# Sigmoid attention and a gated FFN in one kernel: other places for the attention visits, other sums per FFN unit, another order at the start

## The chip, the cores and the metric

One core of a Trainium2 chip. The metric is the device time of one execution in microseconds (us); the profile's span, from the first to the last instruction, is about 1.8 us shorter. A time more than 1.5% above the fastest of the same kernel counts as slow and is left out. In this document PE is the matrix engine, DVE VectorE, ACT ScalarE, POOL GpSimd and SP SyncE.

## The reference

```python
# q, k, v: (8, 12, 448, 64); w_gate, w_val: (768, 1536); w_out: (1536, 768)
scores = q @ k.T / sqrt(64) - log(448)
attn   = sigmoid(scores) @ v                    # per batch and head
x      = attn.transpose(0, 2, 1, 3).reshape(3584, 768)
g      = x @ w_gate
out    = ((g * sigmoid(g)) * (x @ w_val)) @ w_out
```

## The kernel before

Everything is scheduled by hand on one core. Heads are taken four at a time, so there are 24 tile sets n (three in each of eight batches), each with seven score tiles c. A *visit* puts up to four score tiles and the PV product of a finished tile set between FFN units. An FFN1 unit (b, f) is 12 matmuls of 448 columns into the two banks of one PSUM tile, then a gate: sigmoid on ACT, two products on DVE, the last of which writes hT. PSUM is a ring of four such tiles, and a score tile, a PV product or an FFN tile takes the next place in the ring when its last reader is done. FFN2 works on pairs of batches with sums of hT (tiles S) and sums of w_out (tiles wT), so that seven products replace eight; the sums of hT are made on DVE two at a time after each unit of the odd batch.

```python
def ffn1(b, f):
    D = Banked("f", made=(b // 2, f))
    for prs in (range(NP - 2), range(NP - 2, NP)) if f == 0 else (range(NP),):
        ffn1_mm(D, b, f, prs)
    ffn1_gate(D, b, f)               # ACT: s = sigmoid; DVE: t = g * s, hT = val * t
    if b % 2:
        h_sums(b // 2, f)            # puts 1 or 3 sums into a queue
        make_sums(2)                 # does up to two of them
# ... (cut)
visits = [tiles[:2], tiles[2:4]]     # then 3, and from set 4 on 4 + 3 tiles
# ... (cut)
    frac = (j * C + c) / (NJ * C)    # place of a visit within its batch, by tiles
# ... (cut)
def attn_step(group, pvs, how):
    for part in (group[:2], group[2:]):
        scs = [(n, c, qk_tile(n, c)) for n, c in part]               # scores, PE
        rest = [pv(pvs.pop(0), how) for _ in range(len(pvs))]        # PV of the set before
        for i, (n, c, sc) in enumerate(scs):
            sig_tile(n, c, sc, split=len(group) == 4 and part[0] == group[0] and i == 1)
        for f in rest:
            f()
```

Loads, casts to bf16 (POOL, names `c<-st`) and transposes by DMA (`T<-c`) of later tile sets hang on the visits through a table.

## Time and profile before

| | before |
|---|---|
| times at first | 417.18, 417.66, 424.82 us (the last 1.8% above the first: slow) |
| span of the profile | 414.7 us |
| PE / DVE / ACT / POOL busy | 97 / 62 / 51 / 23% |
| first FFN1 matmul, end of the last matmul | 22.33 us, 410.3 us |
| matmuls | 3194 |

The prediction below shows the lines of the page and of the chain. They are read like this: PE holds the chain nearly alone, so only what holds up PE counts; but its busy time also covers waits, so the distance between starts is what has to be compared.

### The profile page before, as it was taken

The page shows a single profiled execution, that of the slowest core. Times are in us where ns is not written, and L with a number is a line of the kernel's source. Part 1 is how long each engine was busy: PE and PEld are TensorE (multiplying, and loading weights), DVE is VectorE, ACT ScalarE, POOL GpSimd, SP SyncE. Part 2 cuts the span into 40 slices and gives each one's busy share as a digit, 9 for nine tenths or more (in the row PEclk, how much of TensorE's full clock was granted, in tenths as well). Part 3 has the DMA queues.
Part 4 walks back from the last instruction along what each step waited for, and adds up shares of the span by engine and source line. Part 5 has one row for each costly group of instructions (what it writes and reads, how often), then busy time and mean ns, then how long its engine had stood idle before and what let it go on. Part 6 is the DMA issues. An engine that isn't in the chain of part 4 may idle for free.

```text
span 414.7 us, 7943 instructions
## 1 busy us (share of the span) xinstructions
PE 403.1 (97%) x3194; PEld 209.9 (51%) x3194; DVE 256.7 (62%) x472; ACT 213.5 (51%) x294; POOL 94.5 (23%) x125
## 2 busy tenths in 40 slices
PE   6799999999999999999999999999999999999995
PEld 3444545545555445445565445445555545555563
DVE  3637557778855555678554555568745447578653
ACT  5966986745444745745704865665715472222000
POOL 5528162446030643200030346020000000000000
PEclk9999999999999999999999999999999999999999
DMA  8999999986779985331374999340025400000135
GB/s 281 238 259 238 220 199 230 216 182 150 192 139 238 197 197 155 67 95 24 62 195 130 200 186 213 86 69 0 2 63 136 114 2 0 2 0 2 38 81 149
DMA packets 59845, 54.39 MB, mean 131 GB/s; under 512 B 35744, under 2 KB 53280, under 8 KB 59808
## 3 DMA queue, kind: packets, MB, share of 16 engines
q0 software_dynamic: 18880, 30.94, 33.9%
q1 hardware_dynamic: 40496, 22.62, 25.5%
q8 instruction: 25, 0.41, 0.4%
q10 hardware_dynamic: 432, 0.33, 0.3%
q14 instruction: 12, 0.10, 0.1%
HBM read 47.19 MB, written 11.01 MB: 140 GB/s over the span
## 4 chain that ended last, share of the span: by engine, by line
PE 89%; ACT 4%; DVE 3%; issue 2%; DMA 1%; POOL 0%; SPq 0%; DVEq 0%; ACTq 0%
PE ps_D L294 51%; PE ps_D L418 18%; PE ps_D L228 8%; PE ps_D L260 6%; PE ps_D L476 5%; ACT pt L246 3%; DMA st<-in_q_dram 1%; PE ps_D L198 1%; DVE S L377 1%; DVE t L314 1%; ACT s L312 0%; DVE hT L318 0%; ACT pt L243 0%; DVE T L204 0%; DVE xT L269 0%
## 5 line engine op out<-in xcount | busy, mean ns | idle before, releaser
L246 ACT ACTIVATE pt<-ps_D,sb_t 128x896 f16<-128x896 f32 x148 | 140.3, 1016 | 84.0 <-PE ps_D L228 79.3
L294 PE MATMUL ps_D<-xT,wg 128*128 128x448 f16 x576 | 126.6, 353 | 0.1
L294 PE MATMUL ps_D<-xT,wv 128*128 128x448 f16 x576 | 126.3, 352 | 0.0
L314 DVE TENSOR_TENSOR t<-ps_D,s 128x448 f16<-128x448 f32 x96 | 59.7, 622 | 74.8 <-ACT s L312 74.4
L312 ACT ACTIVATE s<-ps_D 128x448 f16<-128x448 f32 x96 | 52.6, 548 | 83.4 <-PE ps_D L294 71.2
L294 PEld LDWEIGHTS <-wg 128*128 128x128 f16 x576 | 53.5, 98 | 58.3 <-issue 12.4
L294 PEld LDWEIGHTS <-wv 128*128 128x128 f16 x576 | 56.2, 98 | 52.6 <-issue 0.4
L318 DVE SCALAR_TENSOR_TENSOR hT<-ps_D,t 128x448 f16<-128x448 f32 x96 | 60.0, 625 | 10.0
L179 POOL CAST c<-st 128x896 bf16<-128x896 f32 x41 | 38.2, 941 | 122.0 <-DMA T<-c 63.9
L228 PE MATMUL ps_D<-T,T 64*64 64x448 bf16 x644 | 44.4, 357 | 2.6 <-DVE T L204 1.2
L260 PE MATMUL ps_D<-pt,v 64*64 64x448 f16 x672 | 36.0, 349 | 0.4 <-ACT pt L246 0.3
L429 DVE TENSOR_SCALAR osb<-ps_D 128x384 f32<-128x384 f32 x43 | 24.0, 557 | 19.1 <-PE ps_D L418 18.1
L418 PEld LDWEIGHTS <-S 128*128 128x128 f16 x264 | 25.8, 98 | 17.1
L418 PE MATMUL ps_D<-wT,S 128*128 128x384 f16 x198 | 34.0, 326 | 0.0
L228 PEld LDWEIGHTS <-T 64*64 64x64 bf16 x644 | 15.0, 105 | 25.6 <-issue 19.3
L269 DVE CAST xT<-ps_D 128x448 f16<-128x448 f32 x24 | 14.9, 622 | 20.9 <-PE ps_D L260 15.5
L172 POOL DMA_DIRECT2D v<-in_v_dram x24 | 17.5, 730 | 43.3 <-PE ps_D L228 31.5
L435 DVE SCALAR_TENSOR_TENSOR osb<-ps_D,osb 128x384 f32<-128x384 f32 x33 | 18.4, 557 | 13.5 <-PE ps_D L418 13.5
L274 DVE CAST xT<-ps_D 64x448 f16<-64x448 f32 x42 | 26.1, 621 | 0.7
L260 PEld LDWEIGHTS <-v 64*64 64x64 f16 x672 | 19.8, 107 | 13.0 <-issue 1.0
L418 PEld LDWEIGHTS <-hT 128*128 128x128 f16 x198 | 18.9, 98 | 14.2 <-issue 2.1
L476 PE MATMUL ps_D<-wo,hT 128*128 128x384 f16 x144 | 24.2, 326 | 0.3 <-DVE osb L489 0.3
(45 smaller groups left out, 210.4 us busy)
## 6 DMA issues: line engine op xcount, KB each, us to landing
out_dram<-osb SPq DMA_DIRECT2D x52, 192.0 KB, 2.9
st<-in_q_dram POOLq DMA_DIRECT2D x20, 448.0 KB, 5.4
st<-in_k_dram POOLq DMA_DIRECT2D x20, 448.0 KB, 6.2
v<-in_v_dram POOLq DMA_DIRECT2D x24, 224.0 KB, 7.5
wg<-in_moe_w_gate_dram POOLq DMA_DIRECT2D x4, 576.0 KB, 12.1
wv<-in_moe_w_val_dram POOLq DMA_DIRECT2D x4, 576.0 KB, 13.1
wo<-in_moe_w_out_dram POOLq DMA_DIRECT2D x4, 576.0 KB, 9.4
st<-in_q_dram SPq DMA_DIRECT2D x3, 448.0 KB, 6.1
```

The lines of the kernel that those rows point to most:

```text
L179: eng.tensor_copy(out=t.rearrange("p c h d -> p h c d"), in_=st.rearrange("p h (c d) -> p h c d", c=C))
L228: nc.tensor.matmul(out=sc[w * 64:(w + 1) * 64, h2, :S], lhsT=kt[r, w * 64:(w + 1) * 64], rhs=qt[r, :, w * 64:(w + 1) * 64], start=True, st ...
L246: nc.scalar.activation(out=pt, in_=sc[:, :, :S], func=SIGM, bias=sb_t, scale=qkscale)
L260: nc.tensor.matmul(out=P[g:g + 64, h2, :S], lhsT=vt[r, h2, c * D:(c + 1) * D], rhs=pt[r, h2, :], start=(c == 0), stop=(c == C - 1),)
L274: done = [nc.vector.tensor_copy(out=o, in_=i) for o, i in halves[how:]]
L294: nc.tensor.matmul(out=D.t[:, i, :S], lhsT=(wg16, wv16)[i][f // FW][:, pr, cs], rhs=xT[(b, pr)], start=(pr == 0), stop=(pr == NP - 1),),
L312: D.read(nc.scalar.activation(out=s16, in_=D.t[:, 0, :S], func=SIGM), 0)
L314: D.read(nc.vector.tensor_tensor(out=t1, in0=D.t[:, 0, :S], in1=s16, op=MULT), 0)
L318: nc.vector.scalar_tensor_tensor(out=hT[(b // 2, f)][:, b % 2, :], in0=D.t[:, 1, :S], scalar=HSC, in1=t1, op0=MULT, op1=MULT),
L418: nc.tensor.matmul(out=D.t[:, bank, :hw], lhsT=l, rhs=B_(i), start=(first and i == 0), stop=(i == HF - 1), skip_group_check=True,),
L429: nc.vector.tensor_scalar(out=o, in0=D.t[:, bank, :hw], scalar1=HREC, scalar2=None, op0=MULT), bank
L476: nc.tensor.matmul(out=D.t[:, half, :hw], lhsT=h[:, m * 128:(m + 1) * 128], rhs=wo16[f // FW][:, f % FW, half * hw:(half + 1) * hw], start ...
```

## The change

Its intent: keep PE from waiting at visits. From batch 2 on, visits are spaced evenly and at least two FFN units apart. The number of sums after a unit depends on how far the next visit is: three in the last unit before a visit, none in the last but one before a four-tile visit. In the first FFN1 units, the last two score chunks come earlier.

```diff
-            make_sums(2)
+            make_sums(budget[(b, f)])
...
-        frac = (j * C + c) / (NJ * C)
+        frac = (j * C + c) / (NJ * C) if b == 1 else (j + (0.5 if c else 0.0)) / NJ
...
-    early = [tile_of(0)]
-    ffn1_mm(early[0], 0, 0, four, (0,))
+    early = [tile_of(0), tile_of(2)]
+    ffn1_mm(early[0], 0, 0, range(3), (0,))
     chunk(2, 5, at=(k0 + 3) % 4)
+    ffn1_mm(early[0], 0, 0, (3,), (0,))
     ffn1_mm(early[0], 0, 0, four, (1,))
-    early.append(tile_of(2))
+    chunk(2, 6, at=(k0 + 1) % 4)
     ffn1_mm(early[1], 0, 1, four, (0,))
-    chunk(2, 6, at=(k0 + 1) % 4)
+    pv(2, how=2, at=(k0 + 3) % 4)
     ffn1_mm(early[1], 0, 1, four, (1,))
-    pv(2, how=2, at=(k0 + 3) % 4)
...
-        if vi < len(visits) and tcur >= vtime[vi] and not (was is ffn1 and was_args[1] == 0):
+        if visits and tcur >= vtime[0] and not (was is ffn1 and was_args[1] == 0) and (vtime[0] < FIRST + 4 or since > 1):
...
+            ahead = [len(a) if f is None else 0 for f, a, _ in seq[i + 1:i + 3]] + [0, 0]
+            budget[args] = 3 if ahead[0] else 0 if ahead[1] == 4 else 2
```

Cut: the order is now written into a list first, and the last PV product comes after two units instead of one.

More of the change, by code (lines that the diff above doesn't have):

```diff
@@ L349 @@
     sumq = []
+    budget = {}
     def h_sums(pb, f):
@@ L687 @@
             plan[(n, 4)] += ((fetch, n + 3),)
+    seq = []
     tcur = 3 * FU1
-    vi = 0
-    pend = []
+    since = 99
     was, was_args = ffn1, (0, 2)
     for dur, fn, args in units:
-        if vi < len(visits) and tcur >= vtime[vi] and not (was is ffn1 and was_args[1] == 0):
-            group = visits[vi]
-            vi += 1
+        if visits and tcur >= vtime[0] and not (was is ffn1 and was_args[1] == 0) and (vtime[0] < FIRST + 4 or since > 1):
+            seq.append((None, visits.pop(0), 0 if fn is ffn1 else 1))
+            vtime.pop(0)
+            since = 0
+        seq.append((fn, args, not visits and since == 2))
+        was, was_args = fn, args
+        since += dur > 0.0
+        tcur += dur
+    for i, (fn, args, _) in enumerate(seq):
+        if fn is ffn1:
+            ahead = [len(a) if f is None else 0 for f, a, _ in seq[i + 1:i + 3]] + [0, 0]
+            budget[args] = 3 if ahead[0] else 0 if ahead[1] == 4 else 2
+    pend = []
+    for fn, args, how in seq:
+        if fn is None:
             pvs, pend = pend, []
-            attn_step(group, pvs, 0 if fn is ffn1 else 1)
-            for n, c in group:
+            attn_step(args, pvs, how)
+            for n, c in args:
                 for act, of in plan.get((n, c), ()):
@@ L706 @@
                 trans_pe(post.pop())
-        if pend and (
-            fn is ffn1 and args[1] == 0 and (args[0], NP - 1) not in xT
-            or vi == len(visits) and tcur >= vtime[-1] + 4.0
-        ):
+            continue
+        if pend and (fn is ffn1 and args[1] == 0 and (args[0], NP - 1) not in xT or how):
             for n in pend:
@@ L714 @@
         fn(*args)
-        was, was_args = fn, args
-        tcur += dur
 _INS = ['q', 'k', 'v', 'moe_w_gate', 'moe_w_val', 'moe_w_out']
```

## The prediction

> **What bounds the kernel now.** I read the page first for the busy shares, then the chain that ended last, then the timeline of TensorE (PE) around every place where the chain leaves PE. Page and chain:
>
> ```profile
> PE 403.1 (97%) x3194; PEld 209.9 (51%) x3194; DVE 256.7 (62%) x472; ACT 213.5 (51%) x294; POOL 94.5 (23%) x125
> ...
> PE 89%; ACT 4%; DVE 3%; issue 2%; DMA 1%; POOL 0%; SPq 0%; DVEq 0%; ACTq 0%
> ```
>
> ```profile
> 342.66 43.24 PE ps_D L294 x228
> 385.89 3.90 PE ps_D L476 x24
> 389.79 20.49 PE ps_D L418 x126
> 410.32 0.05 issue
> 410.37 0.56 DVE oe L429
> ```
>
> A busy PE may still be waiting inside its busy time, so I take the distance between starts. In the last 75 us there are no visits (a visit is a batch of attention tiles put between FFN units): 43.24 us / 228 = 0.190 us for a matmul of 448 columns, 20.49 / 126 = 0.163 us for one of 384. Everywhere else in FFN stretches the timeline shows the same pace (an FFN1 unit of 12 matmuls is 2.27 us). So between the first FFN1 matmul (22.33 us) and the last matmul (about 410.3) PE is short of its own pace only inside visits. A normal visit of four tiles, from its first score matmul to the next FFN matmul, lasts 2.21 us (139.96 to 142.17), one of three tiles 0.70 us (134.62 to 135.32). I compared all 43 visits with these. Six are longer:
> - 48.88: 0.86, so 0.16 too long; 52.10: 2.40, 0.19 too long
> - 76.67: 2.33, 0.12 too long
> - 102.00: 1.11, 0.41 too long
> - 171.15: 2.55, 0.34 too long; 235.55: 2.62, 0.41 too long
>
> Together 1.63 us, 0.4% of 414.7. The other losses lie in the first 22 us, where PE waits for the first loads and for scores to pass ScalarE (ACT), and in the last 4 us (eviction and store). The change touches neither.
>
> The 171 visit in the timeline (start, duration, engine, line, tiles, count, idle time before):
>
> ```profile
> 168.52 2.80 ACT L246 ACTIVATE pt<-ps_D,sb_t 128x896 f16<-128x896 f32 x3 [0.92 <-PE ps_D L228]
> ...
> 171.20 0.55 ACT L312 ACTIVATE s<-ps_D 128x448 f16<-128x448 f32 x1
> ...
> 171.55 1.49 PE L260 MATMUL ps_D<-pt,v 64*64 64x448 f16 x28
> ...
> 171.79 0.62 DVE L314 TENSOR_TENSOR t<-ps_D,s 128x448 f16<-128x448 f32 x1 [2.27 <-ACT s L312]
> 172.52 0.62 DVE L318 SCALAR_TENSOR_TENSOR hT<-ps_D,t 128x448 f16<-128x448 f32 x1
> ...
> 173.19 0.57 PE L228 MATMUL ps_D<-T,T 64*64 64x448 bf16 x8
> ```
>
> Only one FFN1 unit lies between this visit and the one before. Its gate sigmoid waits at ACT behind the three score sigmoids until 171.20; VectorE (DVE) then finishes hT at 173.14, and the visit's third score tile, which takes that unit's place in the ring of four PSUM tiles, starts at 173.19. The visit at 235 is the same (hT ends 237.60, scores start 237.66).
>
> **What the Trainium skill says.** "TensorE: Matmul & The Clock Gate", section "Wait — 56ns, not 53.3ns?", gives a warm start-to-start of columns / 2.4 GHz + about 2.5 ns: 189 ns for 448 columns and 162.5 for 384. The trace has 190 and 163, so the FFN stretches have nothing left to give. "Perfetto Trace Analysis", "Identifying the Most-Contended Engine", warns that matmul busy time does not show the distance to the roofline; here the 403.1 us busy contain all six waits above, so the trace agrees. The first page, "Architectural detail", calls ACT and DVE strict FIFO: that is why a sum put ahead of a gate product delays it. The trace agrees: at 76.43 and 76.82 two sums run while the sigmoid for the next product is already done (76.19), and the product starts only at 77.10. "SBUF — State Buffer", section "Who interferes with whom", says that "only the shared port pair causes contention, and it's an exclusive lock"; near 100 us two sums take 0.86 and 1.08 us beside GpSimd casts, alone they take 0.36.
>
> **The change part by part.** No arithmetic, transfer or matmul is added or removed. I wrote out both orders of visits and units by hand from the loops; both have 43 visits.
>
> (a) Visits two units apart. The first seven one-unit gaps (batch 1, early) are kept, because their time lies below the limit in the rule. So the excess at 48.88 and 52.10 stays: 0. Later, the two visits that had only one FFN1 unit ahead of them get two: before, tile sets 12/4-6 and 13/0-3 had one unit between them (this is 168 to 171), and 16/4 and 17/0 (this is 232.5 to 235.5). With two units the first of them has 2.27 us more before its PSUM tile is wanted. In the 171 case hT ends 173.14, while the third tile would then be wanted at about 171.15 + 2.27 + 0.40 + 1.32 = 175.1. The second unit's PSUM tile goes to the PV product or to the third score tile; its sigmoid is no longer behind scores, so it is ready in time too, by 0.5 us if no sum comes in between. Gain 0.34 + 0.41 = 0.75. The one-unit gaps between FFN2 groups (9/4, 22/0) cost nothing before and vanish; a visit moves behind the last group of batches 0/1 and 4/5. The final PV product comes two units instead of one after the last scores: at most 0.04 us.
>
> (b) Sums by distance. In the last but one unit before a four-tile visit no sum is done, in the last one three. That is the cure of the case at 76.67: two sums of 0.36 to 0.39 us stood ahead of the product; without them hT would end 0.75 us earlier than 78.44 and the scores at 78.50 would not wait. Gain 0.12. Other visits in the odd batches have no excess: 0.
>
> But the budget changes what is left over. Counting through batch 1, the queue holds 3 after unit 10 (2 before), so the last unit does 2 and the flush ahead of FFN2 does 4 instead of 3. After the last hT, six sums instead of five stand ahead of the first FFN2 eviction, and this is on the path:
>
> ```profile
> 99.01 0.62 DVE hT L318
> 99.63 0.79 DVE S L377
> 100.42 0.02 issue
> 100.45 1.37 DVE S L377 x2
> 101.82 0.02 issue
> 101.84 0.37 DVE S L377
> 102.21 0.02 issue
> 102.23 0.04 DVE S L377
> 102.27 0.24 issue
> 102.51 0.56 DVE osb L489
> 103.07 0.04 issue
> 103.11 2.92 PE ps_D L476 x17
> ```
>
> PE's next FFN2 tile waits for that eviction, up to 103.11. One sum more, at the pitch of 0.39 us (101.84 to 102.23), makes it 103.50. Loss 0.39. In the pair of batches 4/5 it is also six instead of five, but there a visit and four microseconds of FFN2 lie before the freed tile is wanted; in 2/3 it is four. Neither had a wait, and I expect none: 0.
>
> (c) The early part. Score chunk 5 comes after three instead of four FFN1 matmuls, chunk 6 after eight instead of twelve, PV after twelve instead of sixteen. The timeline has PE without a break from 22.02 to 33.9 already, with every piece at its pace. Moving chunk 6 by 0.76 us shortens an idle time of ACT (0.93 us before 25.62), which is not on the path. By the tile it takes, chunk 5 would be asked for at about 23.0; the sigmoid that frees it ends about 22.9, so no new wait either. The xT copies come about 0.8 us earlier, but they are needed at 29.27 and are done at 28.9 now. Gain 0.
>
> Sum: -0.75 - 0.12 - 0.04 + 0.39 = -0.5 us, rounded; span 414.7 to about 414.2. The two fast times before are 417.18 and 417.66, mean 417.4 (424.82 is 1.8% above and looks like the slower state), so 416.9; I allow 0.2 for something small that I have not seen: 417.1.
>
> **Rivals.**
> 1. Even spacing frees more than I see, and all 1.63 us go: 415.8. For it: the change aims at just these waits. Against it: two of six lie in the stretch whose spacing is kept, and the one at 102 gets worse.
> 2. A delayed visit turns into a late input. Visits late in batches 4 and 6 come up to two units (4.5 us) later, and loads, casts and transposes hang on them. If a transposed tile came late once in each of the three pairs, by 1 us, the time would be 420. Against it: fetch to use still spans more than a whole visit pair, four units and their attention work (about 12 us) between successive transposes, and in the view of waits only one weight load (0.7 us in all, the first PV) names a DMA as what PE waited for. With the page's 5.4 to 7.5 us from issue to landing this is covered.
> 3. The six sums at batch 4/5 or the four at 2/3 meet GpSimd casts and take 1 us each; the eviction of the first FFN2 tile then holds the next visit's fourth tile: +0.5 each, 418. The margin at 2/3 is about 0.7 us, so this is possible.
> 4. The early reorder uncovers a chain at the head: ACT is busy all the time from 10 to 20 us. If chunk 6 a little earlier brought the gates forward, up to 0.5 us. But PE does not idle there, so there is nothing to bring forward.
>
> **Range and chances.** The whole excess that can be removed is 1.63 us (0.4%), so faster by 2% (8.3 us) cannot come from these parts. Slower by 2% needs some twenty waits of 0.4 us; fourteen visits had two units ahead of them before, and the worst of them was 0.12 us too long. Runs of one kernel differ by about 0.5 us. Range 416.0 to 418.4.
>
> **What would show it.** Right: the visits after 12/4 and 16/4 last 2.21 us and not 2.55 and 2.62; the 76.67 visit 2.21; the wait ahead of the second FFN2 tile near 103 grows by 0.4 with six sums before the eviction; 48.88 and 52.10 as before; PE unbroken from 22 to 34. Wrong: score or PV matmuls waiting for casts or transposes, a visit in batches 2 to 6 over 2.3 us, or a first FFN1 gate that starts at another time.

## The result, and the profile after

The kernel after took 415.99 us (median of 6, 415.47 to 416.60), the kernel before 416.78 (median of 6, the three above and 416.21, 416.29, 416.39). The ratio is 0.9982 with a 95% interval of 0.9963 to 1.0001: the same within 2%. A ratio in this document is the mean time of one kernel's fast runs over that of the other's of the same rounds, so not quite the ratio of the medians. The span is 413.7 us instead of 414.7.

Page and end of the chain after (busy share by engine; then start, duration and line of each piece of the chain):

```profile
PE 403.3 (97%) x3194; PEld 210.0 (51%) x3194; DVE 256.3 (62%) x473; ACT 212.5 (51%) x293; POOL 94.2 (23%) x125
...
PE 94%; ACT 3%; DVE 1%; issue 1%; DVEq 0%; ACTq 0%
```

```profile
348.44 36.43 PE ps_D L294 x192
384.87 3.90 PE ps_D L477 x24
388.77 20.49 PE ps_D L419 x126
```

The busy time of PE is the same to 0.2 us, and the pace is too (36.43 / 192 = 0.190 us). Yet the chain lies on PE for 94% instead of 89%: of its detours over ACT and DVE, those of the head and one from 45 to 50 us (ahead of the visit at 49) are left, besides the store at the end. From the first FFN1 matmul to the last matmul's end PE needs 386.7 us (22.59 to 409.24) instead of 387.9 (22.33 to 410.27). That is 1.29 us less. The head is 0.26 us longer, which is no more than it varies by itself: with the old order of the start, the first FFN1 matmul came at 22.33 to 23.34 us in five profiles (that of the kernel before and four of the experiments).

The visit that answers to the one at 171 us before (tile sets 13/0-3), in the chain of the kernel after:

```profile
163.35 0.69 PE ps_D L228 x12
164.04 6.92 PE ps_D L294 x36
170.95 0.50 PE ps_D L228 x8
171.46 1.32 PE ps_D L260 x28
172.78 0.38 PE ps_D L228 x8
173.16 2.94 PE ps_D L294 x15
```

Three units (36 matmuls) now lie ahead of it, where there was one, and it lasts 0.50 + 1.32 + 0.38 = 2.2 us, with no piece on ACT or DVE. The visit at 235 is now at 241.75 and lasts 2.21 us.

The surprise is at 102 us. The prediction had the wait there grow by 0.39 us; it is gone:

```profile
95.93 2.38 PE ps_D L294 x12
98.31 3.90 PE ps_D L477 x24
102.21 0.69 PE ps_D L228 x12
102.90 3.19 PE ps_D L477 x19
```

The timeline of DVE and POOL shows why. After the last hT of batch 1 there are indeed six sums, and the eviction (L490) then waits for PE, not PE for it:

```profile
97.66 0.93 POOL L179 CAST c<-st 128x896 bf16<-128x896 f32 x1 [0.27 <-DMA st<-in_k_dram]
...
99.14 0.62 DVE L318 SCALAR_TENSOR_TENSOR hT<-ps_D,t 128x448 f16<-128x448 f32 x1
99.25 0.72 POOL L167 DMA_DIRECT2D st<-in_k_dram  x1
99.68 0.35 DVE L378 TENSOR_TENSOR S<-hT,hT 128x384 f16<-128x384 f16 x1
...
101.52 0.36 DVE L378 TENSOR_TENSOR S<-hT,S 128x384 f16<-128x384 f16 x1
102.08 1.02 DVE L490 TENSOR_SCALAR osb<-ps_D 128x384 f32<-128x384 f32 x2 [0.21 <-PE ps_D L477]
```

Before, two casts of tile set 10 ran on POOL at 99.28 and 100.47, and two of the five sums took 0.86 and 1.08 us instead of 0.36:

```profile
99.28 0.93 POOL L179 CAST c<-st 128x896 bf16<-128x896 f32 x1 [1.92 <-DMA st<-in_q_dram]
99.55 0.86 DVE L377 TENSOR_TENSOR S<-S,hT 128x384 f16<-128x384 f16 x1
100.45 0.36 DVE L377 TENSOR_TENSOR S<-hT,S 128x384 f16<-128x384 f16 x1
100.47 1.13 POOL L179 CAST c<-st 128x896 bf16<-128x896 f32 x1 [0.26 <-DMA st<-in_k_dram]
100.72 1.08 DVE L377 TENSOR_TENSOR S<-hT,hT 128x384 f16<-128x384 f16 x1
```

Six sums without casts end sooner (2.1 us after the last hT) than five with two (3.0 us). So the questions for the chip are: is it the casts, or the number of sums; and did the change move the casts, or did the loads that the casts wait for just land earlier this time?

### The profile page after: what moved, and what is told of

Its sections match the earlier page's. It is cut to its first block, busy times and chain, and to the rows that moved or that the text cites. A ratio compares the mean times of both kernels' runs of the same rounds, so it can differ in the third digit from the quotient of the medians.

```text
span 413.7 us, 7927 instructions
## 1 busy us (share of the span) xinstructions
PE 403.3 (97%) x3194; PEld 210.0 (51%) x3194; DVE 256.3 (62%) x473; ACT 212.5 (51%) x293; POOL 94.2 (23%) x125
## 4 chain that ended last, share of the span: by engine, by line
PE 94%; ACT 3%; DVE 1%; issue 1%; DVEq 0%; ACTq 0%
PE ps_D L294 53%; PE ps_D L419 18%; PE ps_D L228 8%; PE ps_D L260 7%; PE ps_D L477 6%; ACT pt L246 3%; PE ps_D L559 1%; PE ps_D L198 1%; DVE T L204 0%; ACT pt L243 0%; DVE xT L269 0%; DVE t L314 0%; ACT s L312 0%; DVE oe L430 0%; DVE warm L64 0%
## 5 line engine op out<-in xcount | busy, mean ns | idle before, releaser
L314 DVE TENSOR_TENSOR t<-ps_D,s 128x448 f16<-128x448 f32 x96 | 59.8, 623 | 74.9 <-ACT s L312 74.5
```

Source lines behind the costliest of these rows:

```text
L314: D.read(nc.vector.tensor_tensor(out=t1, in0=D.t[:, 0, :S], in1=s16, op=MULT), 0)
```

## The experiments

Twelve kernels, all with correct output, each run in five timed rounds beside the kernel before, plus the profiled run (so six times each). The first four ran on one chip, the other eight on another. A sum is called stretched when it takes more than 0.4 us (alone it takes 0.36). "Too long" is by how much a visit, from its first score matmul to the next FFN matmul, exceeds the normal 0.70 (three tiles) or 2.21 us (four tiles with PV). The visit at 49 us (0.16 too long) and the next one-unit visit (0.19, at 52) are in every run up to the two that move them, and not listed. The heads of the columns give the times of the visits to within 2 us; they move from run to run.

| run | tile late at 62 | 77 | 95 | sums ahead of the eviction, of these stretched | 102 | 172 | 236 |
|---|---|---|---|---|---|---|---|
| before, first profile | - | 0.12 | - | 5, two | 0.41 | 0.34 | 0.41 |
| after, first profile | - | - | - | 6, none | - | - | - |
| ctrl_before | 0.72 | 0.73 | 0.31 | 5, one | - | 0.34 | 0.40 |
| a_visits | - | 0.12 | - | 5, one | - | - | - |
| b_sums | 1.39 | - | - | 6, none | - | 0.34 | 0.40 |
| c_early | - | 0.28 | 0.42 | 5, one | - | 0.34 | 0.40 |
| after_again | 1.23 | - | - | 6, none | - | - | - |
| ac_nosums | - | 0.12 | - | 5, one | - | - | - |
| after_busy | - | - | - | 6, none | - | - | - |
| before_actcast | - | 0.12 | - | 5, none | - | 0.34 | 0.40 |
| after_busy2 | 1.26 | - | - | 6, two | 0.77 | - | - |
| v_shift | 0.67 | - | - | 6, none | - | - | - |
| v_fetch6 | 1.54 | - | - | 6, none | - | - | - |
| v_both | 1.52 | - | - | 6, one | 0.28 | - | - |

| run | median us | fastest | slowest | ratio to before | 95% interval |
|---|---|---|---|---|---|
| before beside the first four | 417.68 | 416.23 | 419.32 | | |
| ctrl_before | 417.43 | 416.29 | 418.00 | 0.9991 | 0.9964 to 1.0018 |
| a_visits | 416.10 | 415.43 | 417.22 | 0.9967 | 0.9943 to 0.9992 |
| b_sums | 417.32 | 416.22 | 418.02 | 0.9993 | 0.9967 to 1.0019 |
| c_early | 416.91 | 416.61 | 418.63 | 0.9993 | 0.9967 to 1.0018 |
| before beside the next four | 416.78 | 416.22 | 417.90 | | |
| after_again | 416.40 | 415.27 | 417.64 | 0.9993 | 0.9975 to 1.0010 |
| ac_nosums | 416.12 | 415.69 | 417.27 | 0.9988 | 0.9974 to 1.0001 |
| after_busy | 416.14 | 415.61 | 417.50 | 0.9996 | 0.9979 to 1.0013 |
| before_actcast | 417.86 | 416.36 | 418.73 | 1.0022 | 1.0002 to 1.0042 |
| before beside the last four | 416.84 | 416.22 | 417.90 | | |
| after_busy2 | 416.92 | 416.17 | 418.33 | 1.0000 | 0.9984 to 1.0016 |
| v_shift | 416.58 | 415.73 | 417.13 | 0.9993 | 0.9980 to 1.0006 |
| v_fetch6 | 419.53 | 417.20 | 420.45 | 1.0080 | 1.0065 to 1.0096 |
| v_both | 420.07 | 417.34 | 424.41 | 1.0067 | 1.0041 to 1.0092 |

(v_both's 424.41 is slow and not in its ratio.)

**ctrl_before.** The kernel before, no edit.

> The kernel before, unchanged, as a control. All theories: ratio 1.000 within 0.2%; its six long visits show how far the waits move by themselves. Theory A (the wait before the second FFN2 tile near 102 us came from two GpSimd casts that fell on the sums): the casts of tile set 9 start when their loads land, so from run to run they may fall earlier; if both are over before the last hT of batch 1 ends (about 99.6), the five sums take 5 x 0.39 = 1.95 us and the visit at 102 lasts 0.70 instead of 1.11; if they fall on the sums, it stays at 1.0 to 1.2. Rival B (the number of sums ahead of the eviction makes the wait): 1.11 in every run, wherever the casts fall. Rival C (the change itself brings the loads forward): the casts of set 9 start near 99.3 and 100.5 again, not near 96.5 and 97.7 as after.

Measured: 0.9991 (0.9964 to 1.0018): a ratio of these rounds is uncertain by some 0.3%. The visit at 102 was of normal length, with only one stretched sum of five (0.97 us). The wait of 0.41 us that the prediction took for a property of the kernel is not in this run of the same kernel, so rival B (always 1.11) fell. Rival C is not so clear. The first cast of set 10 ran at 99.3 and 99.1 in the two profiles of before. In the four profiles that are the kernel after up to there, but for extra casts some us earlier in one, it ran at 96.5, 97.1, 97.6 and 101.4, so the change does not fix where it falls; that it moves it earlier on the average may be, and is not settled. The control also brought two waits of another kind. The first is a transposed tile of set 6, an input of the scores, that landed late (the timeline names it; the bracket gives the idle time and its releaser):

```profile
63.19 0.57 PE L228 MATMUL ps_D<-T,T 64*64 64x448 bf16 x8 [0.72 <-DMA T<-c]
```

The second shows at 77, where the first profile had only 0.12. Timeline of POOL, DVE and PE:

```profile
77.23 0.94 POOL L179 CAST c<-st 128x896 bf16<-128x896 f32 x1 [0.54 <-DMA st<-in_k_dram]
77.40 0.97 DVE L377 TENSOR_TENSOR S<-hT,hT 128x384 f16<-128x384 f16 x1
...
78.41 0.36 DVE L377 TENSOR_TENSOR S<-S,hT 128x384 f16<-128x384 f16 x1
78.69 0.62 DVE L314 TENSOR_TENSOR t<-ps_D,s 128x448 f16<-128x448 f32 x1
79.41 0.62 DVE L318 SCALAR_TENSOR_TENSOR hT<-ps_D,t 128x448 f16<-128x448 f32 x1
...
80.08 0.57 PE L228 MATMUL ps_D<-T,T 64*64 64x448 bf16 x8 [0.54 <-DVE hT L318]
```

A cast fell on the first of the two sums that stand ahead of a gate product; hT came 0.6 us later than it otherwise does, and the scores that want its PSUM place waited. At 95 the same happened (0.31). These waits come and go with the landing of loads.

**a_visits.** The kernel after without the sums and the early part.

```diff
-            make_sums(budget[(b, f)])
+            make_sums(2)
```

(and the early part of before)

> Only the new places of the visits; two sums per unit as before, early part as before. Theory A: the two visits after a single FFN1 unit (2.55 and 2.62 us) become 2.21, so 0.75 us less than before (ratio 0.9982); the visit at 76.7 stays 0.12 too long; the visit near 102 depends on the casts (0.70 or about 1.1). Rival B: the same 0.75, and the visit at 102 stays 1.11. A rival that even spacing alone frees all of it: all six visits normal, 1.6 us less (0.996).

Measured: the visits at 172 and 236 are normal, the one at 77 is 0.12 too long, just so. The visit at 102 is normal, with one stretched sum. The ratio 0.9967 is lower than 0.9982, which is within its interval; its profile has no late tile. The spacing is most of the gain. The third rival, that it frees everything, fell: 49, 52 and 77 stay.

**b_sums.** Only the sums by distance, on the visits of before.

```diff
-            make_sums(2)
+            make_sums(budget[(b, f)])
```

> Only the sums by distance, on the visits of before. Theory A: the visit at 76.7 becomes 2.21 (-0.12 us), the two visits after single units stay near 2.55 and 2.62, six sums ahead of the FFN2 eviction cost nothing if no cast falls on them (visit near 102 is 0.70) and about 0.4 more than before if both casts do (1.5). Rival B: the visit near 102 lasts 1.11 + 0.39 = 1.5 in either case, so 0.27 us slower than before in all.

Measured: the visit at 77 is normal, those at 172 and 236 are too long as before, and six sums in a row cost nothing (visit at 102 normal), as no cast fell on them: rival B fell again. The ratio 0.9993 hardly says anything, because this profile also has the late tile at 62 (1.39 us). In profiles with the sums by distance (eight of them: both of after, b_sums, both busy runs and the three tries below) the visits at 77 and 95 were never too long; in the six without, 77 always was (0.12 to 0.73) and 95 twice (0.31, 0.42).

**c_early.** Only the new order of the first units, as in the diff of the change.

> Only the early part: chunk 5 after three and chunk 6 after eight FFN1 matmuls. Theory A: TensorE is unbroken from the first FFN1 matmul to the first visit with either order, 11.6 us from the first FFN1 matmul to the first visit's score (22.33 to 33.91 before), so nothing: ratio 1.000 within 0.2%. Rival (the early ScalarE work brings the gates and the waits at 48.9 and 52.1 forward): these two visits shrink by 0.35 us in all, ratio 0.999.

Measured: 11.57 us from the first FFN1 matmul (22.78) to the first visit (34.35), against 11.58 before, and in the kernel after again 11.57 (22.59 to 34.16). The visits at 49 and 52 are as before; ratio 0.9993. The early part does nothing that these runs can show, and the rival fell.

**after_again.** The kernel after, no edit.

> The kernel after, unchanged, against the kernel before with more rounds. The runs so far show a part that varies from run to run in the kernel before too: a transposed tile that lands late near 62 us (0.7 and 1.4 us of wait in two profiles, none in three) and GpSimd casts that fall on sums. Theory A: the fixed gain is 0.34 + 0.41 (visits after a single unit) + 0.12 (sums), so 0.9 us, ratio 0.998, with 0 to 2 us of the varying part on either side; two long visits only after 48 us (0.16 and 0.19), apart from late tiles. Rival: the whole 0.9982 measured was chance of the loads, ratio 1.000.

Measured: 0.9993 (0.9975 to 1.0010). The interval holds both 0.998 and 1.000, so by time alone it does not decide. The profile shows what the theory said: only 49 and 52 too long, and the late tile (1.23 us), which here hit the kernel after. The fastest of six, 415.27, lies 0.95 us under the fastest of eleven runs of before on that chip, 416.22. If the fastest runs are those without late tiles and casts at a bad moment, they compare the fixed part; no profile shows that of these two runs. The profiles themselves give a better measure, the stretch from the first FFN1 matmul to the last matmul's end: less the waits listed in this document, it is 386.3 to 386.4 us in all fourteen. So the list holds all that PE lost there, in every version.

**ac_nosums.** The kernel after with two sums per unit.

```diff
-            make_sums(budget[(b, f)])
+            make_sums(2)
```

> The kernel after with two sums per unit as before (visits and early part new). Theory A: as the kernel after but the visit near 77 is 0.12 us too long, more when a cast falls on a sum there; ratio 0.9983, not to be told from the kernel after. Rival (the sums by distance do most of the work, because they keep sums away from products everywhere): more visits than that one are long, ratio 0.999 to 1.000.

Measured: 0.9988, not to be told from the kernel after, and only 77 is too long (0.12) beyond 49 and 52. The sums by distance do not carry the gain.

**after_busy.** Four extra casts on POOL, into scratch that nothing reads.

```diff
+    def busy(times):
+        for _ in range(times):
+            nc.gpsimd.tensor_copy(out=sc_b, in_=wo16[0].rearrange("p f n -> p (f n)")[:, :2 * S])
...
-        (8, 0): ((ready, 9), (fetch, 10)),
+        (8, 0): ((ready, 9), (busy, 4), (fetch, 10)),
```

> The kernel after with four more GpSimd casts (scratch only, no transfer, output unchanged) right behind the casts of tile set 9, so that GpSimd is busy while the six sums ahead of the first FFN2 eviction run. Theory A (a sum that meets a cast waits for it): three or four of the six sums take 0.8 to 1.1 us instead of 0.36, the eviction starts 1 to 2.5 us later than in the kernel after, the visit near 102 lasts 1.5 to 3 us instead of 0.70, and the kernel is 0.8 to 2 us slower than after (ratio to before 1.000 to 1.003). Rival D (sums were stretched by incoming transfers, not by casts): sums stay at 0.36, visit 0.70, ratio as the kernel after.

This run missed its aim, and the text on record is wrong about the set: the casts near 97 to 100 us belong to set 10, so behind those of set 9 the extra casts ran at 89.7 to 93.6, well before the six sums, which took 0.36 each; the visit was normal. But two earlier sums fell on the extra casts, and took 1.68 us together instead of 0.75:

```profile
89.71 3.93 POOL L596 CAST sc_b<-wo 128x896 bf16<-128x896 f16 x4
91.16 1.68 DVE L378 TENSOR_TENSOR S<-hT 128x384 f16<-128x384 f16 x2
```

These casts only copy what had long been in SBUF, and no load lands for them. So a cast stretches a sum without a transfer of its own, and rival D fell here.

**before_actcast.** The kernel before with the casts of set 9 on ACT, after the last gate sigmoid of batch 1.

```diff
+            o_units.insert(1, (0.0, lambda n: casts_act(n), (9,)))
...
-        (8, 0): ((ready, 9), (fetch, 10)),
+        (8, 0): ((fetch, 10),),
```

> The kernel before with the two casts of tile set 9 on ScalarE instead of GpSimd, placed after the last gate sigmoid of batch 1. Theory A: no GpSimd cast is left near the five sums, they take 0.36 each (0.39 pitch), the visit near 102 lasts 0.70 instead of 1.11; 0.41 us faster than the first profile of before, nothing against runs of before in which the casts fell elsewhere. Rival B (number of sums): five sums still cost the 0.41 us, visit 1.11. The waits of 0.34 and 0.40 near 172 and 236 stay in either case.

The same mistake about the set, but here it worked, by another way: set 10's loads were issued only after ACT had freed their staging (POOL waited 8.3 us for ACT), so set 10's casts came at 105.8, and no cast was near. Five sums took 0.36 each, the visit at 102 was normal, and 172 and 236 stayed. The ratio, 1.0022, is slower than before all the same. The profiled run (417.36) begins FFN1 at 23.34, 1.0 us later than the first profile of before; what its three runs over 418 us waited for is in no profile and stays open.

**after_busy2.** The same four extra casts behind those of set 10.

```diff
-        (8, 4): ((casts, 10),),
+        (8, 4): ((casts, 10), (busy, 4)),
```

> The run after_busy put its four extra GpSimd casts at the wrong place: they ran at 89.7 to 93.4, before the sums (the casts near 97 to 100 belong to tile set 10, not 9). Here the same four follow the casts of set 10. Theory A (a sum that meets a GpSimd cast waits for it): the extra casts run from about 99.5 to 103.5, several of the six sums take 0.8 to 1.1 us instead of 0.36, the eviction starts 1 to 2.5 us late, the visit near 102 lasts 1.5 to 3 us instead of 0.70, so the fast end of the times rises from 415.3 to 416.3 or more. Rival D (transfers stretch the sums): sums 0.36, visit 0.70, fast end 415.3 to 415.7.

Measured: chance did the work, since set 10's own casts came late and fell on the sums, and the extra ones fell on the eviction and what follows:

```profile
101.44 1.05 POOL L179 CAST c<-st 128x896 bf16<-128x896 f32 x1 [2.67 <-DMA st<-in_q_dram]
101.73 0.97 DVE L378 TENSOR_TENSOR S<-S,hT 128x384 f16<-128x384 f16 x1
...
103.53 1.02 POOL L179 CAST c<-st 128x896 bf16<-128x896 f32 x1 [1.04 <-DMA st<-in_k_dram]
103.79 0.97 DVE L378 TENSOR_TENSOR S<-hT,S 128x384 f16<-128x384 f16 x1
...
105.28 0.97 PE L477 MATMUL ps_D<-wo,hT 128*128 128x384 f16 x5 [0.71 <-DVE osb L490]
```

Two of six sums stretched, and PE waits 0.71 us for the eviction: the visit lasts 1.47 instead of 0.70. That is a little short of the 1.5 to 3 expected, since two sums met casts and not four. The visit at 113, after the last extra casts, was 0.40 too long as well. These casts start when a load lands, so this run by itself does not tell casts from transfers (rival D); after_busy does. In the kernel after, moreover, POOL issued loads right among the six sums (99.25 to 100.7) and none stretched. And in all fourteen profiles 37 sums start while a POOL cast runs: 36 of them end 0.20 to 0.21 us after that cast and take up to 1.12 us (the other started 0.01 us before the cast's end). The 1307 that start beside no cast take 0.34 to 0.36 us. The fast end of the times rose to 416.17.

Put together, the wait at 102, by number of sums and how many met a cast (the 0.77 is of after_busy2, with its extra casts; the eviction there still took 0.54 us, as long as elsewhere):

| | none | one | two |
|---|---|---|---|
| five sums | 0 (1 profile) | 0 (4 profiles) | 0.41 (1) |
| six sums | 0 (6) | 0.28 (1) | 0.77 (1) |

**v_shift.** The visits of batch 1 start one unit earlier, against the waits left at 49 and 52.

```diff
-            vtime.append(4 * FU1 + frac * (FIRST + 1.0 - 4 * FU1))
+            vtime.append(3 * FU1 + frac * 17.2)
```

> A try at the two waits that the change leaves (0.16 and 0.19 us at two visits of batch 1 with one FFN1 unit between them): batch 1's visits begin one unit earlier, which gives the visit of tiles 5/0-3 two units ahead of it. Theory A: the 0.19 goes, the 0.16 stays or moves, all the rest as after: 0.2 us faster than after at most, not to be told apart by time, only by the visits in the profile. Rival: an earlier start asks for the transposed tiles of sets 4 and 5 too early, and TensorE waits 0.5 us or more for their casts.

Measured: one wait of 0.15 stays (47.4), the 0.19 goes, but a new 0.15 appears at the next one-unit visit (57.5), and the first visit, now at 32.2, is 0.24 too long. No gain: 0.9993, as after_again.

**v_fetch6.** The loads of set 6 ahead of the last two weight loads.

```diff
     w_load("v", 2)
+    load(6, 0, G)
+    load(6, 1, G)
     load_v(5)
...
-        (4, 0): ((fetch, 6),),
+        (4, 0): ((load_v, 6),),
```

> A try at the varying wait: the loads of q and k of tile set 6 are issued ahead of the last two weight loads instead of behind them. Theory: the late transposed tile near 62 us (0.7, 1.4 and 1.3 us in three of the profiles so far, none in the others) goes, because its casts run 5 to 8 us earlier; the slow end of the times falls from 417.6 to about 416.5, the fast end stays at 415.3 (ratio to before 0.997). Rival: the weights of FFN1 units 9 to 11 come late instead and TensorE waits there, or the transposes themselves take as long as before.

Measured: 0.8% slower, the clearest result of all, and the opposite of the aim. The casts of set 6 did come 6.8 us earlier (43.1 instead of 49.9), but POOL then issued the next loads 6.8 us earlier too, and the second transpose of set 6, issued at 45.5 instead of 52.3, took 18.6 us to land instead of 7.6: it landed at 64.1 instead of 59.8. That the loads delayed it is my reading of this profile; no run tests it. The tile was 1.54 us late:

```profile
64.17 0.57 PE L228 MATMUL ps_D<-T,T 64*64 64x448 bf16 x8 [1.54 <-DMA T<-c]
```

The profiled run was the fastest of the six (417.20); what made four others take 419 to 420 us I have not seen.

**v_both.** Both edits.

> Both tries together. If each does what it should: no late tile near 62, one long visit of 0.16 left after 48 us, fast end 415.1, slow end 416.4, ratio to before 0.9965. If the earlier visits need tiles that the moved loads delay, slower than v_fetch6 alone.

Measured: 1.0067, slower like v_fetch6, with the early waits of v_shift (0.23, 0.16 and 0.15). Its profile gave the one case of six sums with a single stretched one (1.08 us): 0.28 at 102. No version beat the kernel after.

## Why the prediction was right or wrong

The time, 415.99, sits at the lower end of the stated range (416.0); the class was right. The number expected inside it, 417.1, was 1.11 too high: 0.62 because 417.4, the mean of two runs, was taken for the kernel before (the median of six is 416.78, and the profile it was subtracted from, with 414.7 of span and 1.8 outside it, was a run of 416.5), 0.2 for the reserve, and 0.29 for the change itself (-0.79 instead of -0.5). By its own steps:

- **What bounds the kernel** (six long visits, 1.63 us to be had): right for the profile that it read: without these waits its stretch from 22 to 410 us is 386.3 us long, as in every other profile to 0.1 us, and the gain stayed under the ceiling of 0.4%. (The 189 and 162.5 ns that it sets beside the pace are estimates by the formula of the page it cites; the trace has 190 and 163.) But the list was read from one execution, as if it were the kernel. In fourteen profiles four of the six were there whenever the code was the same (49, 52, 172, 236); 77 was there but changed its size (0.12 to 0.73), and 102 came once in the two profiles of before. Two of its counts are off, without effect: six one-unit gaps are kept in batch 1, not seven, and eleven visits had exactly two units (24 matmuls) ahead of them, not fourteen. After the change the visit of 13/0-3 has three units ahead of it, not two.
- **(a) Visits, 0.75 us**: right, to the 0.01 us. 0.34 and 0.40 to 0.41 in all five profiles with the old spacing, zero in all nine with the new. The 0.04 for the last PV product was not there: its 1.45 us before next to 1.45 after.
- **(b) Sums, 0.12 us gained at 77**: right in the mechanism, too small. What it keeps away from the product is not two sums of 0.36 but two sums that may each meet a cast. The waits that it is there to remove were 0.12 where none did, and 1.04 in ctrl_before (0.73 + 0.31), 0.70 in c_early (0.28 + 0.42).
- **(b) Sums, 0.39 us lost at 102**: this is the step that failed. The counts were right (six sums, and six and four in the later pairs), the cost was not. "One sum more, at the pitch of 0.39 us (101.84 to 102.23), makes it 103.50" kept the two stretched sums of that execution fixed. With two stretched it is right: 0.77 instead of 0.41, a difference of 0.36. With none, the sixth sum ends 0.2 us before PE lets the eviction begin, and costs nothing. With one it is 0.28 instead of 0. So the sixth sum is a cost that depends on where the casts fall, and the change carries it. The view had the cause in it, and the prediction named it (0.86 and 1.08 us beside casts) without asking whether the casts would be there the next time; each cast waits for a load, as the bracket at its line says.
- **(c) Early part, 0**: right.
- **Rival 2, a late input**: it was set aside with the argument that hardly a PE wait named a DMA. In half of the profiles one did, at 62 us, 0.67 to 1.54 us, in both kernels alike (0.72 in ctrl_before, 1.23 in after_again), so it is no effect of the change. The prediction called it covered by the median landing times of the loads (5.4 to 7.5 us); the transposes of the same profile between 36 and 66 us took 3.1 to 12.5. The late tile is one part of the spread of the times; the start of FFN1, at 22.33 to 23.53 us, is another.
- **Rivals 1, 3 and 4**: 1 (all 1.63 us go) fell, since 49 and 52 stay; that 102 was normal in the first profile of after looks like it, but was the luck of the casts. 3 (the sums of the later pairs meet casts, and a visit waits) was not seen: no visit near 201 or 301 us was long in any profile, and near 301 POOL has no work left. 4 fell with (c).

The sum of what the first two profiles differ by: 0.12 + 0.41 + 0.34 + 0.41 = 1.28 us of the 1.29 measured between the first FFN1 matmul and the last matmul's end. Of this 0.87 is fixed. It is also what lies between the stretches of before_actcast (387.53), where no cast fell on sums at 77, 95 or 102 and no tile was late, and of the kernel after (386.66); and it agrees with the difference of the fastest runs (416.22 - 415.27 = 0.95). The 0.41 is luck. Whether the mean gain is nearer to 0.07% or 0.18% the rounds do not settle; the intervals of both comparisons hold both values.

## What to carry to other kernels

A wait read off one profile is only a property of the kernel if nothing in its chain hangs on a transfer's landing; where an engine's line carries a DMA as its releaser, take a second profile before counting on the wait or on its absence. When an engine shares a path with another, keep work that can be put off away from the instruction that frees a buffer: the worth is larger than the plain durations say. An earlier load is not a gain by itself: in v_fetch6 it made POOL issue the next loads 6.8 us earlier, and a transpose then took 18.6 us to land instead of 7.6.

## What the Trainium skill lacked or had wrong

- "SBUF — State Buffer", "Who interferes with whom": it says that a DVE instruction with two SBUF inputs contends with a POOL instruction that reads SBUF, and that the second to start blocks fully. The runs agree in kind: the sums (two SBUF inputs) stretched, the 253 gate products that started during a cast did not (0.61 to 0.63 us, as the others), and the 95 sums that started while POOL issued a load took 0.35 to 0.36. No number is given for this pair; here 36 sums that started during a cast ended 0.20 to 0.21 us after the cast's end, which is less than the 0.36 a sum takes alone, and a cast that began while a sum ran took 0.93 to 1.13 us (18 cases; 0.93 to 0.97 with DVE idle).
- "DMA: Bandwidth & Descriptors", section "DMA Transpose (X-bar)", gives no time from issue to landing on busy engines; here it was 3.1 to 11.8 us in the kernel after and 6.7 to 18.6 in v_fetch6, between 36 and 66 us.
- "TensorEngine Tiling (Array Packing)", "Key Properties", says that a change of tiling mode drains the engine, without a cost; here a visit of 12 score matmuls lasts 0.70 us, of which four at a time (as the 28 PV matmuls run, 1.32 us) would take 3 x 0.19 = 0.57. That leaves about 0.13 us for the two changes together, an estimate from these durations; no run separates the changes from other causes.
